# Ranking the products of Z C v with the first layer's weights in front of the next batch's attention

## The chip, the core and the metric

The kernel runs on one core of a Trainium2 chip. The metric is the device time of one execution in microseconds (us), the median of several runs. The engines are TensorE (PE in the rows, its weight loads PEld), VectorE (DVE), ScalarE (ACT), GpSimd (POOL) and SyncE (SP), which issues the DMA transfers. Every engine takes its instructions in the order in which the program lists them, and an instruction whose input is not there holds up all behind it.

## The reference

```python
C = sm(q_lm, k)                       # 32 landmarks per head
Z = iterated inverse of Bm            # 6 steps
attn = A @ Z @ C @ v                  # 4 batches, 8 heads, 576 x 64
x = attn.transpose(0, 2, 1, 3).reshape(2304, 512)
xn = x / sqrt(mean(x * x) + 1e-6) * rms_g
x = (silu(xn @ w_gate) * (xn @ w_val)) @ w_out    # 512 -> 1536 -> 512
# then a mixture of 8 experts, taken by the rows with x @ w_skip > 0
```

## The kernel before

The kernel never forms the attention's output. For a batch it computes the small matrix Z C v (32 landmarks by 64, for 8 heads), transposes it, scales it by `rms_g` and keeps it as `WT`. It multiplies `WT` with the first layer's weights: `product` makes a tile `P` of 128 x 512 for two groups of heads, which then plays the part of the weights, while the normed rows of A (`ap_t`) play the part of the activations. All large matrix products run in three pieces of split numbers (high part and low part, `rsplit`): for `P` ACT casts the PSUM bank to the high part and DVE subtracts it to get the low part.

The hidden layer is cut into thirds of 512 columns. A batch has six products: here g0, v0, g1, v1, g2, v2, for gate (g) and value (v) of thirds 0 to 2. Each takes 16 matmul instructions (32 in the trace, two passes each) on a quarter-sized piece of the array, 64 rows by 32 columns; `manual_schedule` fixes their order among themselves, so that eight pieces run side by side. Its results fill the two PSUM banks of the pool `pb`, which serve also the small steps `lp`, `lg` and `x2t` of the unit before. So the next product waits until both casts and both subtractions of the one before are done.

Its weights come through `load_w`: four DMA transfers of 256 KB on SP's queue, into the tiles `wl` (gate) or `wr` (value). There are two tiles of each, so the load of the next third waits until PE has finished the product with this one.

The main loop runs over eight units, two halves of 288 rows for each of four batches. A unit goes through 12 pieces of the hidden layer (`pg`, `pv`, 6 matmuls each, thirds 0 to 2 of `P` four pieces each), and then 144 matmuls of the output projection (`o`). Side work is woven in through generators: the next batch's attention (`attention`, from a batch's first half on), the products of the next batch (`products`, queued from piece 4 of the second half), and `finish` of the unit before. The steps of the attention that the prediction names are `gram`, `sq` (both the product with `gram` and, in the following batch, the scores), `ms`, `rbs` (the rows' norm: ACT takes a square root, which needs a table load on ACT), `ap` and `ap_t` (normed rows, split), then for the batch after that `s`, `lmk`, `bdq` (landmarks, on DVE), `pb`, `sq`, `mx`, `C`, `cT`, `sk`, `pv` with `vt`. Tanh for `h` needs ACT's other table.

What sets the final order on each engine is a scheduler that picks, among the instructions that it takes to be ready, the one of best rank. The rank is the place at which the program wrote it. I call the passage from one batch to the next a boundary: the first one lies at about 200 to 250 us, the second at 308 to 350, the third at 420 to 470.

Of the kernel before, what the change touches and what calls it, by code (L numbers as in the profile page):

```python
# [29 lines left out]
ROUND = 1.5 * 2.0**23  # L30
LP = 40
NC0 = 5
SLACK = 700


# [27 lines left out]
def attention_moe_kernel(  # L63
# [16 lines left out]
    def rsplit(lo_eng, hi, lo, src):  # L80

        A.copy(hi, src)
        lo_eng.tensor_tensor(lo, src, hi.bitcast(F32), ALU.subtract)
# [58 lines left out]
    def bank(name):  # L142
        return pb.tile([128, 512], F32, name=name, tag="b")
# [615 lines left out]
    def convert_w(i):  # L759

        load_raw(i)
        w = wo_tile(F32)
        from_f64(w, raws[i], wtile("s64"))
        for a in (1, 2):
            load_raw(i + a)
        SP.dma_start(parts_at(w_d[PARTS[i][0]], i), w)
        wparts[PARTS[i]] = w
# [13 lines left out]
    def load_w(n, q, last=False):  # L781

        ws = []
        for c in range(2):
            if n == "g" or last:
                w = wtile("wl").rearrange("p c n -> p (c n)")
            else:
                w = raw.tile([128, DM, 2], F32, name="wr", bufs=2)
                w = w.rearrange("p c n -> p (c n)")
            w = w.rearrange("p (i n) -> p i n", n=PC)  # L790
            f = DM * q + PC * c
            for g in range(2):
                SP.dma_start(
                    w[64 * g : 64 * g + 64],
                    w_d[n][256 * g : 256 * g + 256, f : f + PC].rearrange(
                        "(i p) n -> p i n", p=64
                    ),
                )
            ws.append(w)
        wparts[n, q] = ws  # L800
# [4 lines left out]
    def ptile(n, g, q):  # L805
        i = PIECES.index((n, g))
        return P_t[q][:, i, 0], P_t[q][:, i, 1]

    def product0(q, n, g):

        ps = bank("P")
        w = wparts.pop((n, g, q))
        for p in range(2):
            PE.matmul(
                ps[64 * p : 64 * p + 64, :], WTs[0][:, g, p],
                w[:, p], start=True, stop=True,
            )
        hi, lo = ptile(n, g, q)
        rsplit(V, hi, lo, ps)

    def product(b, q, n):

        pss = [bank("P") for g in range(2)]
        ws = wparts.pop((n, q))

        with tc.manual_schedule(engines={nc.tensor.engine}):
            for c in (1, 0):  # L830
                for i in range(KC):
                    for g in (1, 0):
                        gs = slice(64 * g, 64 * g + 64)
                        PE.matmul(
                            pss[g][32 * i : 32 * i + 32, PC * c : PC * c + PC],
                            WTs[b][gs, i], ws[c][gs, i], start=True, stop=True,
                        )
        for g, ps in enumerate(pss):
            hi, lo = ptile(n, g, q)
            rsplit(V, hi, lo, ps)  # L840

    def products(b, q):

        if b == 0:
            for n, g in PIECES:
                product0(q, n, g)
                yield
            return
        last = b == B - 1 and q == NQ - 1
        for n in "g" if last else "gv":  # L850
            if (n, q) not in wparts:
                load_w(n, q)
        for n in "gv":
            product(b, q, n)
            if last and n == "g":
                load_w("v", q, last)
                yield
            elif n == "g" and q < NQ - 1:
                load_w(n, q + 1)
            yield  # L860
# [167 lines left out]
    def pair_at(lst, i):  # L1028
        return ld(lst, i, E - 1), ld(lst, i + LP, B - 1)
# [156 lines left out]
    def slot():  # L1186
# [3 lines left out]
        for g in side[:]:  # L1190
            if max(busy[n] for n in "VAG") > busy["P"] + SLACK:
                break
# [47 lines left out]
    def first_convs():  # L1240
        for i in range(NC0):
            convert_w(i)
            yield
# [22 lines left out]
    ptile_q(1)  # L1266
    h_t = pool(ph1, "h_p").tile([128, FC, 2, NH], F32R, name="h_t")
    drain(products(0, 0))
    late_constants()
    fast = False  # L1270
# [4 lines left out]
    def conversions():  # L1275
        for i in range(NC0, 12):
            convert_w(i)
            yield
            if i == 7:
                drain(products(0, 1))  # L1280
                yield
        nonlocal raw
        start1.close()
        raw = pool(pha, "raw", side="right")
        ptile_q(2)
        drain(products(0, 2))
        yield
        side.append(att)
        for f in range(FC):
            convert_wout(f)  # L1290
            yield
# [24 lines left out]
    for u in range(1, 2 * B):  # L1316
        b, half = u // 2, u % 2
# [60 lines left out]
    with tc.For_i(0, npairs) as i:  # L1378
        e, b = pair_at(rest[0], i + 1)
# [36 lines left out]
```

## Time and profile before

| | us |
|---|---|
| median of 3 runs (711.12 to 711.8) | 711.46 |
| the profiled execution | 710.12 |
| its span, first to last instruction | 708.4 |
| PE busy | 650.1 (92%) |
| DVE busy | 459.8 (65%) |
| ACT busy | 295.4 (42%) |
| POOL busy | 145.1 (20%) |
| mean granted share of TensorE's clock | 0.96 |

A time of the profile is one execution's; the median of the runs is 1.34 above that execution. Busy PE is not PE at its best: a lone small matmul counts as busy while it runs through the array with nothing beside it.

### The profile page before, as it was taken

Reading aid. Unit: us, or ns where it says so; the run is one execution under the profiler, and the core shown is the slowest. Engines: PE = TensorE matmul, PEld = TensorE weight load, DVE = VectorE, ACT = ScalarE, POOL = GpSimd, SP = SyncE. Lnnn points to the kernel's source line nnn. Section 1 sums busy time; section 2 is a strip of 40 time slices with the busy share of each in tenths; the row PEclk is TensorE's granted clock in tenths of the full one; section 3 lists DMA queues with packets and bytes.
Section 4 is the critical chain, followed back from the end, with each engine's and each line's share of the span. In section 5 each row is a group of like instructions: output and inputs, shape, how many; then the busy total and the mean of one; then the engine's idle time right before and its main releaser. Section 6 shows DMA issues by size and latency. Waiting matters only on the chain.

```text
span 708.4 us, 13179 instructions
## 1 busy us (share of the span) xinstructions
PE 650.1 (92%) x4895; PEld 561.1 (79%) x4895; DVE 459.8 (65%) x1030; ACT 295.4 (42%) x637; POOL 145.1 (20%) x162
## 2 busy tenths in 40 slices
PE   5368599798998899999999999999989999999997
PEld 5256177687986598978899887999889988988985
DVE  5995999979877596878368768261452554352451
ACT  0873888834324431443341335240452244242340
POOL 4000035213200140220040030040372024022120
PEclk9775799999998999999999999999999999999999
DMA  8686644762238543428522108230451275445454
GB/s 295 229 256 223 218 148 160 215 171 83 67 95 182 123 111 86 132 64 201 134 66 68 66 20 170 67 73 1 161 153 64 60 234 197 150 130 175 134 158 147
DMA packets 79439, 97.17 MB, mean 137 GB/s; under 512 B 16016, under 2 KB 58000, under 8 KB 79376
## 3 DMA queue, kind: packets, MB, share of 16 engines
q1 hardware_dynamic: 79376, 96.33, 46.2%
q8 instruction: 39, 0.64, 0.4%
q14 instruction: 24, 0.20, 0.1%
HBM read 76.97 MB, written 19.34 MB: 136 GB/s over the span
## 4 chain that ended last, share of the span: by engine, by line
PE 70%; DVE 16%; DMA 4%; ACT 3%; issue 3%; POOL 2%; SPq 1%; POOLq 0%; ACTq 0%; DVEq 0%
PE o L58 17%; PE py L58 11%; PE ph L58 11%; PE pv L58 9%; PE pg L58 8%; PE P L58 3%; PE sq L58 3%; DVE wo L58 3%; PE nr L58 2%; DVE h L58 2%; DVE rbs L58 2%; DVE P L58 1%; PE sk L58 1%; DMA kq<-in_q_dram 1%; DVE ap L58 1%
## 5 line engine op out<-in xcount | busy, mean ns | idle before, releaser
L58 PE MATMUL o<-h_t,wo 128*128 128x288 f32 x1152 | 168.1, 301 | 6.5 <-ACT wo L58 3.6
L58 PEld LDWEIGHTS o<-h_t,wo 128*128 128x128 f32 x1152 | 157.3, 190 | 15.5 <-issue 5.9
L58 POOL TENSOR_TENSOR h_t<-h,h_t 128x288 fp32r<-128x288 f32 x96 | 81.6, 853 | 366.1 <-ACT h_t L58 343.8
L58 PE MATMUL pg<-ap_t,P 128*128 128x288 f32 x576 | 101.1, 305 | 10.8 <-ACT P L58 7.9
L58 PE MATMUL pv<-ap_t,P 128*128 128x288 f32 x576 | 102.4, 306 | 2.5 <-DVE h L58 2.1
L58 PEld LDWEIGHTS pg<-ap_t,P 128*128 128x128 f32 x576 | 83.1, 190 | 22.9 <-issue 14.8
L58 PEld LDWEIGHTS pv<-ap_t,P 128*128 128x128 f32 x576 | 83.8, 191 | 8.7 <-DVE h L58 4.3
L58 PE MATMUL ph<-xsh,P 128*128 128x288 f32 x384 | 78.1, 296 | 0.0
L58 DVE SCALAR_TENSOR_TENSOR h<-h,pg 128x288 f32<-128x288 f32 x96 | 42.6, 446 | 33.8 <-ACT h L58 33.2
L58 PEld LDWEIGHTS ph<-xsh,P 128*128 128x128 f32 x384 | 62.0, 188 | 0.6 <-issue 0.5
L58 ACT ACTIVATE h<-pg 128x288 f32<-128x288 f32 x96 | 39.2, 410 | 49.1 <-PE pg L58 46.4
L58 PE MATMUL ph<-xsl,P 128*128 128x288 f32 x192 | 56.9, 296 | 0.0
L58 ACT CAST h_t<-h 128x288 fp32r<-128x288 f32 x96 | 41.2, 431 | 30.2 <-DVE h L58 29.7
L58 PE MATMUL py<-wo,h_t 128*128 128x512 f32 x210 | 51.7, 397 | 0.0
L58 DVE TENSOR_TENSOR h<-h,pv 128x288 f32<-128x288 f32 x96 | 42.5, 446 | 7.7 <-PE pv L58 5.0
L58 PEld LDWEIGHTS py<-wo,h_t 128*128 128x128 f32 x210 | 39.5, 188 | 9.6
L58 DVE STREAM_TRANSPOSE T<-kq 64x576 f32<-64x576 f32 (+1 forms) x40 | 35.5, 887 | 5.1 <-DMA kq<-in_k_dram 4.0
L58 PEld LDWEIGHTS ph<-xsl,P 128*128 128x128 f32 x192 | 36.0, 188 | 0.1
L58 DVE TENSOR_TENSOR P<-P,P 128x512 fp32r<-128x512 f32 x48 | 31.6, 681 | 6.8 <-ACT P L58 6.5
L58 POOL TENSOR_TENSOR P<-w1r,P 128x512 fp32r<-128x512 f32 x16 | 21.2, 1329 | 69.0 <-ACT P L58 66.9
L58 ACT CAST P<-P 128x512 fp32r<-128x512 f32 x48 | 26.3, 587 | 21.7 <-PE P L58 21.1
L58 DVE TENSOR_SCALAR x2T<-o 128x288 f32<-128x288 f32 x16 | 7.3, 456 | 40.6 <-PE o L58 40.5
(235 smaller groups left out, 954.5 us busy)
## 6 DMA issues: line engine op xcount, KB each, us to landing
wl<-wg_d SPq DMA_DIRECT2D x36, 256.0 KB, 4.6
wr<-wv_d SPq DMA_DIRECT2D x32, 256.0 KB, 4.9
w1r<-in_moe_w_dram SPq DMA_DIRECT2D x32, 256.0 KB, 3.3
wr<-in_moe_w_gate_dram SPq DMA_DIRECT2D x6, 1024.0 KB, 6.3
wr<-in_moe_w_val_dram SPq DMA_DIRECT2D x6, 1024.0 KB, 5.9
wo<-in_moe_w_dram SPq DMA_DIRECT2D x24, 256.0 KB, 5.0
kq<-in_k_dram SPq DMA_DIRECT2D x8, 576.0 KB, 4.4
kq<-in_q_dram SPq DMA_DIRECT2D x8, 576.0 KB, 4.1
```

The lines of the kernel that those rows point to most:

```text
L58: return f(*args, **kw)
```

## The change

The two lines around `product` in `products` rank all that a product issues as though it had been written 150 places earlier. That holds for its matmuls, casts and subtractions. The loads of weights stay outside of the block. The first batch's products take another path and are not touched.

```diff
+AHEAD = 150
...
         for n in "gv":
-            product(b, q, n)
+
+            with tc.high_priority(offset=AHEAD):
+                product(b, q, n)
             if last and n == "g":
                 load_w("v", q, last)
                 yield
```

No instruction is added or taken away. What moves is shown for the places that the prediction speaks of.

First boundary, PE, from the norm of the second batch (`ms`) to its first hidden pieces. `P<-wl` is a gate product, `P<-wr` a value product; x16 is a whole one. Before:

```order
L58 MATMUL ms<-sq,onesd 128x288 x2
L58 MATMUL o<-h_t,wo 128x288 x2
L58 MATMUL P<-wl,WT 32x256 x16
L58 MATMUL o<-h_t,wo 128x288 x54
L58 MATMUL pg<-ap_t,P_675 128x288
L58 MATMUL P<-wl,WT 32x256 x16
L58 MATMUL pg<-ap_t,P_675 128x288 x5
L58 MATMUL P<-wr,WT 32x256 x16
L58 MATMUL pb<-lmk_2544,bdq 64x32 x2
L58 MATMUL sq<-T,bdq 64x288
L58 MATMUL pv<-ap_t,P_675 128x288 x2
```

After (two lone matmuls of g0 stand further ahead, in front of each pair of `sq`):

```order
L59 MATMUL P<-wl,WT 32x256 x14
L59 MATMUL o<-h_t,wo 128x288 x3
L59 MATMUL ms<-sq,onesd 128x288 x2
L59 MATMUL o<-h_t,wo 128x288 x44
L59 MATMUL P<-wl,WT 32x256 x16
L59 MATMUL o<-h_t,wo 128x288 x11
L59 MATMUL P<-wr,WT 32x256
L59 MATMUL o<-h_t,wo 128x288 x2
L59 MATMUL P<-wr,WT 32x256 x15
L59 MATMUL o<-h_t,wo 128x288 x10
L59 MATMUL pg<-ap_t,P_675 128x288 x6
```

g0 moves in front of `ms` and is cut in three; g1 and v0 move from the first hidden piece into the projection, and v0 is cut in two. On ACT the same place reads, before:

```order
L58 ACTIVATE x2T<-o 128x288
L58 ACT_TABLE_LOAD
L58 ACTIVATE rbs<-rbs,eps 128x288 x2
L58 CAST P_675<-P 128x512 x2
L58 CAST ap_t<-ap 128x288 x3
```

And after:

```order
L59 ACTIVATE x2T<-o 128x288
L59 CAST P_675<-P 128x512 x2
L59 ACT_TABLE_LOAD
L59 ACTIVATE rbs<-rbs,eps 128x288 x2
L59 CAST ap_t<-ap 128x288 x2
L59 CAST P_679<-P 128x512 x2
```

The table load and the square root now stand behind the casts of g0, and the casts of g1 between those of `ap_t`.

First boundary, PE, some 15 us later: the scores of the third batch's attention, with v1, g2 and v2. Before:

```order
L58 MATMUL sq<-T,bdq 64x288 x3
L58 MATMUL P<-wr,WT 32x256 x16
L58 MATMUL cT<-ident,C 96x128 x6
L58 MATMUL P<-wl,WT 32x256
L58 MATMUL sk<-T,bdk 64x288
L58 MATMUL P<-wl,WT 32x256 x15
L58 MATMUL sk<-T,bdk 64x288 x3
```

After:

```order
L59 MATMUL sq<-T,bdq 64x288
L59 MATMUL P<-wr,WT 32x256 x16
L59 MATMUL sq<-T,bdq 64x288 x3
L59 MATMUL P<-wl,WT 32x256 x16
L59 MATMUL cT<-ident,C 96x128 x6
L59 MATMUL lp<-x2T,wcat 32x288 x4
L59 MATMUL sk<-T,bdk 64x288 x4
```

v1 moves into the scores, and g2 follows it with only three `sq` between; g2 is whole again. The subtractions of v1 on DVE stand behind two reductions `mx` of these `sq`.

Second boundary, PE, g0 to g1. Before (two lone matmuls of g0 stand ahead of this, in front of two runs of `sq`):

```order
L58 MATMUL P<-wl,WT 32x256 x14
L58 MATMUL pg<-ap_t,P_984 128x288 x3
L58 MATMUL ms<-sq,onesd 128x288 x2
L58 MATMUL pv<-ap_t,P_984 128x288
L58 MATMUL P<-wr,WT 32x256
L58 MATMUL pv<-ap_t,P_984 128x288 x5
L58 MATMUL o<-h_t,wo 128x288 x3
L58 MATMUL P<-wr,WT 32x256 x15
L58 MATMUL o<-h_t,wo 128x288 x28
L58 MATMUL P<-wl,WT 32x256
L58 MATMUL o<-h_t,wo 128x288 x8
L58 MATMUL P<-wl,WT 32x256 x15
```

After:

```order
L59 MATMUL P<-wl,WT 32x256 x16
L59 MATMUL gram<-GT 128x128
L59 MATMUL sq<-AT,gram 128x288 x2
L59 MATMUL pg<-ap_t,P_984 128x288 x2
L59 MATMUL P<-wr,WT 32x256
L59 MATMUL pg<-ap_t,P_984 128x288
L59 MATMUL pv<-ap_t,P_984 128x288
L59 MATMUL P<-wr,WT 32x256 x15
L59 MATMUL sq<-AT,gram 128x288 x2
L59 MATMUL pv<-ap_t,P_984 128x288 x5
L59 MATMUL o<-h_t,wo 128x288 x14
L59 MATMUL P<-wl,WT 32x256 x16
```

g0 and g1 are whole now, v0 is still cut in two, and g1 stands closer behind g0. Behind this v1, cut in two before, is whole, and v2, whole before, is cut in two. The third boundary changes in the same way, except that v1 was whole there already.

## Rows read from the trace of the kernel before

**Rows 1.** The page's head

```profile
span 708.4 us, 13179 instructions
```

**Rows 2.** Busy time by stretch: stretch and length, then engine busy (x instructions), clock, DMA

```profile
180.00:240.00 60.00, 56.31 (x500) 45.91 (x500) 42.56 (x92) 20.32 (x49) 5.11 (x6) 0.94 0.49 120
...
300.00:360.00 60.00, 59.73 (x549) 50.13 (x548) 41.83 (x97) 24.14 (x56) 9.87 (x13) 1.00 0.55 131
...
420.00:480.00 60.00, 59.38 (x551) 50.45 (x550) 36.18 (x77) 23.86 (x56) 11.27 (x14) 1.00 0.40 92
```

**Rows 3.** The same view of three short stretches of the first boundary

```profile
218.90:221.70 2.80, 1.02 (x19) 0.47 (x25) 2.80 (x7) 2.02 (x3) 0.00 (x0) 1.00 0.99 299
221.80:228.50 6.70, 6.13 (x43) 4.38 (x29) 3.32 (x11) 1.51 (x5) 0.00 (x0) 0.50 1.02 210
...
235.00:237.50 2.50, 1.83 (x10) 0.84 (x10) 1.66 (x4) 2.08 (x6) 0.00 (x0) 1.00 0.75 195
```

**Rows 4.** Timeline of PE, first boundary: start, length, operation [idle before, releaser]

```profile
220.71 2.20 PE L58 MATMUL P<-wr,WT 64*32 64x256 f32 x32 [1.78 <-DVE P L58]
223.47 0.43 PE L58 MATMUL pb<-lmk,bdq 128*64 128x32 f32 x4 [0.57 <-DVE bdq L58]
...
234.96 1.01 PE L58 MATMUL cT<-ident,C 128*96 128x128 f32 x6 [0.48 <-ACT C L58]
236.64 0.62 PE L58 MATMUL P<-wl,WT 64*32 64x256 f32 x2 [0.67 <-DVE P L58]
```

**Rows 5.** Timeline of PE, second boundary

```profile
311.25 0.62 PE L58 MATMUL P<-wl,WT 64*32 64x256 f32 x2
311.79 1.24 PE L58 MATMUL sq<-AT,gram 128*128 128x288 f32 x4
...
323.65 0.62 PE L58 MATMUL P<-wl,WT 64*32 64x256 f32 x2
324.20 1.33 PE L58 MATMUL o<-h_t,wo 128*128 128x288 f32 x8
325.46 1.09 PE L58 MATMUL P<-wl,WT 64*32 64x256 f32 x30
```

**Rows 6.** Timeline of PE, third boundary

```profile
435.16 0.59 PE L58 MATMUL P<-wl,WT 64*32 64x256 f32 x2 [0.45 <-DMA wl<-wg_d]
...
440.86 1.09 PE L58 MATMUL P<-wr,WT 64*32 64x256 f32 x32
441.89 12.93 PE L58 MATMUL o<-h_t,wo 128*128 128x288 f32 x95
```

**Rows 7.** Timeline of SP's issues, second and third boundary

```profile
314.92 2.88 SPq L793 DMA_DIRECT2D wl<-wg_d  x4
...
425.93 2.60 SPq L793 DMA_DIRECT2D wl<-wg_d  x4
```

**Rows 8.** DMA issues, last of each of these four: count, size, us to landing

```profile
wl<-wg_d SPq DMA_DIRECT2D x1, 256.0 KB, 4.5
...
wl<-wg_d SPq DMA_DIRECT2D x1, 256.0 KB, 7.1
```

**Rows 9.** Groups by line: busy, mean ns of one, idle before and releaser

```profile
L58 DVE TENSOR_TENSOR P<-P,P 128x512 fp32r<-128x512 f32 x48 | 31.6, 681 | 6.8 <-ACT P L58 6.5
...
L58 ACT CAST P<-P 128x512 fp32r<-128x512 f32 x48 | 26.3, 587 | 21.7 <-PE P L58 21.1
```

**Rows 10.** Timeline of DVE, first boundary

```profile
233.00 0.94 DVE L58 TENSOR_REDUCE mx<-sq 128x1 f32<-128x288 f32 x2 [3.35 <-PE sq L58]
```

**Rows 11.** Timeline of ACT, first and second boundary

```profile
202.19 1.28 ACT L58 ACT_TABLE_LOAD   x1
208.26 1.02 ACT L58 ACTIVATE rbs<-rbs,eps 128x288 f32<-128x288 f32 x2 [4.79 <-DVE rbs L58]
...
316.74 1.28 ACT L58 ACT_TABLE_LOAD   x1
318.04 0.96 ACT L58 ACTIVATE rbs<-rbs,eps 128x288 f32<-128x288 f32 x2
```

## The prediction

> **What bounds the kernel now.** I read the busy times by stretch first. From the first boundary on PE is the bound: it is busy for 59.73 of 60 us around the second boundary and 59.38 around the third, at full clock [rows 2]. So at these two no more than 0.27 and 0.62 us of idle time can be won, and anything beyond that must come from PE doing the same work more densely. The first boundary is different: 56.31 of 60 us, at a mean clock of 0.94 [rows 2]. The short stretches say where. Between 218.9 and 221.7 us PE is busy for 1.02 of 2.80 us; from 221.8 to 228.5 its granted clock is 0.50, the lower level of 1.2 GHz, while it is busy for 6.13 of 6.70 us [rows 3]. The timeline names the waits: v0 starts after 1.78 us of idle time that ended with DVE's subtraction of g1, and `pb` after 0.57 us, waiting for DVE's landmarks [rows 4]. The products and the landmarks of the attention after next meet on DVE there, and PE stands still. That is the place at which the order can matter.
>
> **The change, first boundary.** What goes: g1 and v0 now stand in the projection, where other work runs while their banks are emptied. The idle 1.78 and 0.57 us go [rows 4]. If PE is busy before it, the clock doesn't fall; work of 6.13 us at half clock takes half at full clock, so 3.05 us go at most [rows 3]. Together 5.4.
>
> What comes, in four steps. (1) Cuts. A lone first matmul of a product takes 0.54 to 0.55 us from its start to the next instruction's (311.25 to 311.79, 323.65 to 324.20), and the rest of the product still takes what a whole one does: 1.03 for a whole one (440.86 to 441.89) [rows 5, 6]. The eight `o` behind it take 1.26 (324.20 to 325.46) and not 8 x 0.136 = 1.09, with 12.93 / 95 = 0.136 for one in a long run [rows 5, 6]. So a cut costs about 0.7. This boundary had one (g2) and gets three (two in g0, one in v0): 2 x 0.7 = 1.4. (2) v0 behind g1. An evacuation is two casts of 0.59 on ACT and two subtractions of 0.68 on DVE [rows 9]; the first bank is free 1.3 us after the product at the earliest, and between stand 11 `o`, 1.5 us. But ACT and DVE now take `ap_t` first, and that comes later than before: the table load ran at 202.19, hidden, 4.8 us before its square root at 208.26 [rows 11]; now it stands behind g0's casts, and the square root comes 1.5 to 2 us later. Walking down DVE's queue from there I get the first subtraction of g1 about 1.0 us after PE asks for the bank. Bounds 0 and 2.0. (3) `pv` of the first hidden piece needs the low part of v0. Ten `o` and six `pg` stand between, 2.2 us, against casts, subtractions and a few DVE steps of normed rows and landmarks: 0.6, bounds 0 and 1.5. (4) g2 close behind v1. Before, `cT` and g2 waited 0.48 and 0.67 us [rows 4]. Now DVE does `mx` twice (0.94) and two subtractions (1.36) before both banks are free [rows 9, 10], 2.3 us, while three `sq` give PE about 1 us of work: some 1.35 of waiting, and 0.8 for `lp`, which needs a bank of g2. That is 1.0 more than the 1.15 before; bounds 0 and 2.2. SP's queue loses nothing that PE waits for here: the `vt` loads behind the weights are wanted later.
> The sum is -5.4 + 1.4 + 1.0 + 0.6 + 1.0 = **-1.4**, between -5 and +1.7.
>
> Here a page speaks against the change. In the trace the square root starts 0.02 us after the table load of 1.28 us ends (316.74 + 1.28, 318.04) [rows 11]. The Trainium skill (ScalarE: Activation LUTs, What ACT_TABLE_LOAD costs) adds a drain of about 1.38 us to each switch, 2.66 in all. By that, step (2) would cost 2.4 and the whole change would save 2.7 us and not 4.05; these rows show no such drain, and I stay with 1.28.
>
> **Second boundary.** Before, it has five cuts (two in g0, one each in v0, g1 and v1), after it two (v0 and v2): -3 x 0.7 = -2.1. With the idle 0.27 us gone, -2.4. What may come is a wait for weights. The load of g1 starts when g0 frees its tiles: before, at 314.92; the last of the four transfers, issued some 0.65 before the end of their 2.88 us, at about 317.2, landed 4.5 later, at 321.7, that is 6.8 after the first issue [rows 7, 8]. Between g0 and g1 PE now has 23 full matmuls (23 x 0.136 = 3.1), four `sq` (two in at most 1.24 [rows 5], so about 2 for four), a `gram` (about 0.3) and the cut v0 (1.03 + 0.7): some 7.1 us, and g0 ends about 0.25 after the first issue. By this boundary's own landing that is just in time; by the third's it is 1.8 too early. I take 0, and keep 1.8 for the range. The table load and the `ap_t` chain are later here too, but the hidden pieces that need them still stand behind g2 and 72 `o`, 72 x 0.136 = 9.8 us, so they cost nothing; that cover gone, the 1.5 to 2 us of step (2) would show.
> **-2.4**, between -3.0 and -0.6.
>
> **Third boundary.** Four cuts become two: -1.4, and the 0.62 us of idle time [rows 2], 0.45 of them the wait for g1's weights [rows 6], go or are replaced. The weights: first issue at 425.93, the last at about 427.9, landed after 7.1, so 9.1 after the first issue, and indeed PE waited until 435.16 [rows 6 to 8]. The same 23 matmuls and small steps stand before g1 now, so PE asks 1.75 too early. I take this boundary's own landing: -1.4 - 0.6 + 1.75 = **-0.25**, between -2.0 and +0.5.
>
> All other instructions keep their order, and PE is busy behind each boundary, so what is won stays won. The sum is -1.4 - 2.4 - 0.25 = -4.05. Against the profiled execution's own time, 710.12 (708.4 of span [rows 1] and 1.7 around it), that is 706.1; the runs' median lies 1.34 above, so 707.4 for the median.
>
> **The rivals.**
> *Evacuation takes the place of order.* The four waits of the first boundary come out at their upper ends: products that follow each other closely wait for each other's casts and subtractions, which take 1.2 and 1.4 us against 1.03 on PE. Steps (2) to (4) cost 5.7 and not 2.6: 707.4 + 3.1 = 710.5, no change that can be told. For it: the largest wait of this boundary, 1.78 us, was one for a subtraction [rows 4]. Against it: all but v1 and g2 have now 1.5 us or more of other work between them. The Trainium skill (TensorEngine Tiling (Array Packing), PSUM Bottleneck) says that emptying PSUM may become the bound once small tiles run side by side; this is that case.
> *The clock falls at new waits: slower.* Before the fall at 221.8 PE had been idle for 1.78 of 2.80 us, with a narrow product behind [rows 3, 4]. Now g2's wait of 1.35, with `lp`'s 0.8 soon after, and the third boundary's wait of 1.75 for weights, with narrow products behind each, look much the same. One fall costs what the old one did, 3.05 us: 710.45. Two falls cost 6.1: 713.5, slower. It decides from two falls on, that is, if both waits reach about 1.8 us. Against it: between 235.0 and 237.5 PE was busy for 1.83 of 2.50 us, among narrow products, and the clock stayed at 1.00, the level of 2.4 GHz [rows 3].
> *The waits don't come.* DVE and ACT are ahead of my walk and the weights land in 6.8 us everywhere: steps (2) to (4) near 0.5 in all and no wait at the third boundary, 707.4 - 2.1 - 1.75 = 703.5.
> That the change does nothing is ruled out by the order.
>
> **How the numbers follow.** A measurement of this kernel can tell some 0.2% from no change, that is 710.04 to 712.88 for none. Forecast (705 to 709.5): 0.55. No waits (702 to 705): 0.12. Evacuation or one fall (710 to 711.5): 0.20, a fourth of it still below 710.04. Two falls or more, or the upper ends together: 0.13. So faster 0.72, same 0.15, slower 0.13. The range from 702.5 to 711.5 leaves out the slower case and the far end of the best one.
>
> **What would show it.** In the profile after: no clock of 0.50 around 220 to 230 us; v0's wait of 1.78 gone, and waits of about 1 us for DVE's `P` in the projection's end and at g2; no lone product matmuls among `sq` at the second and third boundary, and g0, g1 in one piece of about 1.03 us there; a wait of some 1.7 us for `wl` at the third. Wrong would be: a half clock at a new place, waits of DVE's `P` over 2 us, or a table load of ACT with PE waiting for `ap_t` behind it.

## The result and the profile after

| | before | after |
|---|---|---|
| median of the runs (8 each), us | 711.00 (706.74 to 711.80) | 703.98 (701.33 to 705.49) |
| ratio, 95% interval | | 0.9905 [0.9884, 0.9926] |
| the profiled execution, its span | 710.12, 708.4 | 704.12, 702.4 |

The change makes the kernel faster by 0.95%, about 6.75 us (the two medians are 7.02 apart). The prediction was 4.05 us and 707.4 for the median; its range, 702.5 to 711.5, holds the time, but its main case, 705 to 709.5 with a chance of 0.55, does not: 703.98 lies in the case without waits, which had 0.12. Two more measurements, on two chips and each beside its own runs of before, gave 0.9895 [0.9859, 0.9930] and 0.9902 [0.9868, 0.9936]. Here is the head of the page of after, with the line on PE, and the groups that answer to [rows 9].

```profile
span 702.4 us, 13192 instructions
...
PE 646.1 (92%) x4895; PEld 561.4 (80%) x4895; DVE 457.9 (65%) x1030; ACT 296.4 (42%) x637; POOL 144.6 (21%) x162
```

```profile
L59 DVE TENSOR_TENSOR P<-P,P 128x512 fp32r<-128x512 f32 x48 | 31.4, 687 | 1.6 <-ACT P L59 1.4
...
L59 ACT CAST P<-P 128x512 fp32r<-128x512 f32 x48 | 26.2, 588 | 22.3 <-PE P L59 21.8 <-DVE ap_t L59 0.3
```

PE is busy for 4 us less than before (650.1) with the same work: three cuts fewer, and no half clock at the first boundary. The evacuations take what they took; what went is idle time of DVE in front of the subtractions, from 6.8 to 1.6 us.

Busy time in the first stretch of [rows 2]:

```profile
180.00:240.00 60.00, 57.20 (x578) 45.81 (x574) 45.29 (x100) 21.89 (x53) 5.42 (x7) 1.00 0.55 131
```

PE is busy for 0.89 us more there and the clock is 1.00 throughout, where it was 0.94.

**Where the time went.** To divide it up I take a step that has the same place in all kernels, `lg` in every other unit, from the timeline of PE; here before, then after.

```profile
185.91 0.77 PE L58 MATMUL lg<-ident,h 128*128 128x9 f32 x6
...
288.04 0.67 PE L58 MATMUL lg<-ident,h 128*128 128x9 f32 x6
...
400.03 0.67 PE L58 MATMUL lg<-ident,h 128*128 128x9 f32 x6
...
502.86 0.67 PE L58 MATMUL lg<-ident,h 128*128 128x9 f32 x6
```

```profile
186.67 0.77 PE L59 MATMUL lg<-ident,h 128*128 128x9 f32 x6
...
285.15 0.67 PE L59 MATMUL lg<-ident,h 128*128 128x9 f32 x6
...
395.03 0.67 PE L59 MATMUL lg<-ident,h 128*128 128x9 f32 x6
...
496.43 0.67 PE L59 MATMUL lg<-ident,h 128*128 128x9 f32 x6
```

The three distances between them hold one boundary each. The table gives them for every kernel that was profiled (one execution each), and the timed ratio beside them. b_again is the kernel before once more, a_again and a_third are the changed kernel once more; the others are explained below.

| kernel | 1st boundary, us | 2nd, us | 3rd, us | ratio to before, 95% |
|---|---|---|---|---|
| before | 102.13 | 111.99 | 102.83 | 1 |
| b_again | 102.15 | 111.96 | 102.56 | |
| after | 98.48 | 109.88 | 101.40 | 0.9905 [0.9884, 0.9926] |
| a_again | 98.44 | 109.95 | 101.06 | 0.9895 [0.9859, 0.9930] |
| a_third | 98.49 | 109.46 | 100.80 | 0.9902 [0.9868, 0.9936] |
| e1_batch2 | 98.45 | 112.54 | 102.57 | 0.9957 [0.9935, 0.9978] |
| e2_batch34 | 102.67 | 110.25 | 102.02 | 0.9959 [0.9933, 0.9985] |
| e3_evac | 100.34 | 112.52 | 103.33 | 1.0019 [0.9995, 1.0043] |
| e4_matmul | 98.47 | 110.73 | 104.04 | 0.9960 [0.9933, 0.9987] |
| c_late500 | 101.48 | 109.88 | 101.27 | 0.9945 [0.9921, 0.9969] |
| s_ahead75 | 98.49 | 132.99 | 114.28 | 1.0302 [1.0260, 1.0343] |
| s_ahead600 | 95.51 | 109.60 | 101.62 | 0.9886 [0.9851, 0.9922] |
| s_q01 | 96.95 | 108.50 | 101.07 | 0.9844 [0.9810, 0.9878] |
| s_q01_2 | 95.50 | 108.54 | 101.30 | 0.9868 [0.9834, 0.9902] |

The two profiles of before agree within 0.3 us, the three of after within 0.6. By their means the first boundary gave 3.67 us (102.14 to 98.47), the second 2.21 and the third 1.61, 7.5 in all. The profiled pair alone gives 3.65, 2.11 and 1.43. The prediction had 1.4, 2.4 and 0.25: the second boundary was right, the first and third were too low. What lies outside the three distances is 1.2 us longer in the profile of after than in that of before; in the five profiles of the two kernels it lies anywhere between 389.3 and 393.8 us, so a single execution's whole span says less than these distances.

Busy time between the four marks, before:

```profile
185.91:288.04 102.13, 97.20 (x880) 81.85 (x881) 76.80 (x180) 32.55 (x84) 13.49 (x16) 0.97 0.48 120
288.04:400.03 111.99, 111.72 (x1011) 96.86 (x1010) 81.57 (x196) 41.41 (x106) 21.23 (x26) 1.00 0.41 105
400.03:502.86 102.83, 102.21 (x900) 92.02 (x899) 54.37 (x129) 34.34 (x88) 19.25 (x24) 1.00 0.27 67
```

And after:

```profile
186.67:285.15 98.48, 95.55 (x881) 80.22 (x881) 76.01 (x180) 32.92 (x84) 13.09 (x16) 1.00 0.50 125
285.15:395.03 109.88, 109.65 (x1011) 96.87 (x1010) 80.46 (x196) 41.33 (x106) 21.26 (x26) 1.00 0.42 106
395.03:496.43 101.40, 100.64 (x901) 92.22 (x899) 54.04 (x129) 34.89 (x88) 19.24 (x24) 1.00 0.29 68
```

At the first boundary PE's idle time fell from 4.93 to 2.93 us and its busy time from 97.20 to 95.55, at a clock of 1.00 where it was 0.97. At the other two there was hardly any idle time to win. What they gained is busy time, by denser work at an unchanged clock: 2.07 us for three cuts less and 1.57 for two, 0.69 and 0.79 a cut (a cut is a place at which other matmuls stand inside a product).

First boundary, timeline of PE, after; it answers to [rows 4]:

```profile
215.60 1.09 PE L59 MATMUL P<-wl,WT 64*32 64x256 f32 x32
...
218.94 0.62 PE L59 MATMUL P<-wr,WT 64*32 64x256 f32 x2 [0.59 <-DVE P L59]
...
233.63 1.69 PE L59 MATMUL P<-wl,WT 64*32 64x256 f32 x32 [1.19 <-issue]
...
236.75 0.69 PE L59 MATMUL lp<-x2T,wcat 128*32 128x288 f32 x8 [0.64 <-DVE P L59]
...
242.37 0.77 PE L59 MATMUL lg<-ident,h 128*128 128x9 f32 x6 [0.27 <-DVE P L59]
```

These are g1, the lone first matmul of v0, g2, and the two small steps that need a bank behind g2. PE's waits in this stretch are 0.59 + 1.19 + 0.64 + 0.27 = 2.69 us; no wait of `pv` for v0 stands there. For g2 the profile names no releaser; the timeline of DVE has the two subtractions of v1 in front of it:

```profile
232.85 1.28 DVE L59 TENSOR_TENSOR P<-P,P 128x512 fp32r<-128x512 f32 x2
```

The first of them (0.68 us) ends at 233.53 and g2 begins at 233.63; the second ends at 234.13. Until then g2 stands still, and PE counts as busy: its row is 1.69 us long, where a whole product's is 1.09. In before v0 stood in the same way inside its row of 2.20 us [rows 4]; the rest of that length is the half clock. Here are the matmuls of `P` alone in the first 0.6 us, of v0 before and of g2 after:

```profile
220.70:221.30 0.60, 0.59 (x2) 1.00 0.95 234
```

```profile
233.60:234.20 0.60, 0.57 (x2) 1.00 1.14 247
```

Two of 32 run in it, 25 in the first 0.6 us of a product that waits for nothing (g1 of before, from 216.97). So 0.6 us of waiting is hidden in busy time at each of these two places.

### The profile page after: what moved, and what is told of

Its sections match the earlier page's. It is cut to its first block, busy times and chain, and to the rows that moved or that the text cites. A ratio compares the mean times of both kernels' runs of the same rounds, so it can differ in the third digit from the quotient of the medians.

```text
span 702.4 us, 13192 instructions
## 1 busy us (share of the span) xinstructions
PE 646.1 (92%) x4895; PEld 561.4 (80%) x4895; DVE 457.9 (65%) x1030; ACT 296.4 (42%) x637; POOL 144.6 (21%) x162
## 4 chain that ended last, share of the span: by engine, by line
PE 72%; DVE 14%; DMA 4%; ACT 4%; issue 3%; POOL 1%; SPq 1%; ACTq 0%; POOLq 0%; DVEq 0%
PE o L59 18%; PE py L59 11%; PE ph L59 11%; PE pv L59 9%; PE pg L59 7%; PE P L59 3%; PE sq L59 3%; DVE wo L59 3%; PE nr L59 2%; DVE h L59 2%; DMA kq<-in_q_dram 1%; PE sk L59 1%; DVE rbs L59 1%; PE x2t L59 1%; DVE P L59 1%
## 5 line engine op out<-in xcount | busy, mean ns | idle before, releaser
L59 DVE SCALAR_TENSOR_TENSOR h_t<-ph,h_t 128x288 fp32r<-128x288 f32 (+2 forms) x45 | 14.6, 353 | 28.9 <-ACT h_t L59 28.9
```

The source lines that it names most:

```text
L59: return f(*args, **kw)
```

## The experiments

A product in three pieces has two cuts; before has 10 of them in the three boundaries (1, 5, 4), after 7 (3, 2, 2).

### One boundary without the others

The rank for the second batch alone (first boundary), and for the third and fourth alone (second and third boundary):

```diff
-            with tc.high_priority(offset=AHEAD):
+            with tc.high_priority(offset=AHEAD) if b == 1 else nullcontext():
```

> The rank only for the second batch's products, so only the first boundary (200 to 250 us) is changed; the second and third keep the order of before. Theory T (what the comparison of the two profiled runs says: the first boundary gave 3.6 us, the second 2.1, the third 1.4): 3.6 us less than before, a ratio near 0.995, about half of the whole gain of 6.7 to 7 us. The prediction's own sum for this boundary: 1.4 us less (ratio 0.998). Rival A, the change works through the second and third boundary alone and the first boundary's difference is drift between two executions: no difference, ratio 1.000.

```diff
-            with tc.high_priority(offset=AHEAD):
+            with tc.high_priority(offset=AHEAD) if b > 1 else nullcontext():
```

> The rank only for the third and fourth batch's products: the second and third boundary as in the changed kernel, the first as before, with its idle 1.78 us in front of the first third's value product and the half clock behind it. Theory T: 3.5 us less than before (2.1 + 1.4), ratio 0.995, and the first boundary's stretch at the half clock is there as before. The prediction's own sum: 2.65 us less. Rival A: all of the 6.7 to 7 us, ratio 0.9905. With the first kernel of this call: the two gains add up to the whole one if the boundaries do not act on each other.

Measured: 0.9957 and 0.9959 of 708.87, so 3.05 and 2.9 us less, each with an interval of about 1.5 to 2 us on either side. Together 6 us, so the boundaries add up, and half of the gain is the first one's; it is no drift. In the profiles the first kernel has after's length in the first boundary and before's in the others, the second the reverse, all within some 0.6 us.

### What of the rank does it: evacuations or matmuls

Only the casts and subtractions ranked ahead:

```diff
-        for g, ps in enumerate(pss):
-            hi, lo = ptile(n, g, q)
-            rsplit(V, hi, lo, ps)
+        with tc.high_priority(offset=AHEAD):
+            for g, ps in enumerate(pss):
+                hi, lo = ptile(n, g, q)
+                rsplit(V, hi, lo, ps)
```

> Only the evacuations (the casts and subtractions) are ranked ahead by 150, the products' matmuls keep the place of before. TensorE's order at the first boundary is that of before, so the products' cuts stay. Theory T: the evacuation of the first third's gate product no longer stands behind the landmark inverse's work on VectorE, so the idle 1.78 us and the half clock (3.05 us) go, and what waits for the landmarks pays about 1 us: 3 to 4 us less than before at the first boundary, nothing at the other two, ratio about 0.995. Rival B (the place of the matmuls carries the gain, the evacuations follow it): no difference, ratio 0.999 to 1.001. Rival C (evacuations in front hold up the attention that TensorE waits for next): slower by 1 to 2 us.

Only the banks and matmuls:

```diff
-        pss = [bank("P") for g in range(2)]
+        with tc.high_priority(offset=AHEAD):
+            pss = [bank("P") for g in range(2)]
...
-            with tc.high_priority(offset=AHEAD):
-                product(b, q, n)
+            product(b, q, n)
```

(the matmuls stand in the block too, the casts and subtractions don't)

> Only the products' matmuls and their banks are ranked ahead, the casts and subtractions keep the rank of before, so TensorE's order is about that of the changed kernel, with few cuts, but the first third's gate evacuation stands behind attention work on VectorE again. Theory T: the second and third boundary give their 3.5 us, the first boundary keeps its wait for a free bank (now earlier in the order, 2 us or more, as evacuations are later against the matmuls than before) and perhaps the half clock: 2 to 3.5 us less than before, ratio 0.995 to 0.997. Rival B (the place of the matmuls carries the gain): 6.7 us less, ratio 0.9905.

The evacuations' rank alone gives nothing: 1.0019 [0.9995, 1.0043]. My expectation fell here. The timeline of PE in e3_evac shows why: the wait in front of v0 is there, as long as before.

```profile
219.30 2.56 PE L59 MATMUL P<-wr,WT 64*32 64x256 f32 x32 [1.79 <-DVE P L59]
```

DVE's order in front of that wait is that of before: the better rank didn't bring g1's subtractions forward, probably because the scheduler doesn't take them to be ready any earlier (not shown). So the rank of the evacuations is not what removed the wait; what another place of theirs would do, this kernel doesn't test.

The matmuls' rank alone gives 0.9960. That is the time I expected, but not for the reason I gave: I had the gain at the second and third boundary and none of it at the first. In the profile the first boundary has the whole of it, 98.47 against 98.48. There it needs no help:

```profile
216.43 0.62 PE L59 MATMUL P<-wr,WT 64*32 64x256 f32 x2 [0.59 <-DVE P L59]
...
424.14 1.22 PE L59 MATMUL P<-wl,WT 64*32 64x256 f32 x32 [0.61 <-DMA wl<-wg_d]
...
432.69 0.66 PE L59 MATMUL o<-h_t,wo 128*128 128x288 f32 x3 [0.76 <-ACT h_t L59]
433.85 3.73 PE L59 MATMUL o<-h_t,wo 128*128 128x288 f32 x26 [0.50 <-POOL h_t L59]
```

In the second boundary it is 0.85 to 1.3 us behind after (one cut more, in v1), in the third 2.6 to 3.2: there `o` waits 1.26 us for `h_t`, and PE is idle for 2.61 us in all against 0.76 after. So the evacuations' rank is worth having, but only at the two later boundaries and only beside the matmuls' rank.

### Putting the wait back

After, with g1's evacuation at the first boundary ranked late, so that its second subtraction stands behind the landmarks:

```diff
-        for g, ps in enumerate(pss):
-            hi, lo = ptile(n, g, q)
-            rsplit(V, hi, lo, ps)
+        late = b == 1 and (n, q) == ("g", 1)
+        with tc.high_priority(offset=-500) if late else nullcontext():
+            for g, ps in enumerate(pss):
+                hi, lo = ptile(n, g, q)
+                rsplit(V, hi, lo, ps)
```

> The changed kernel, but at the first boundary the evacuation of g1 (the second product) is ranked 350 behind the program's order, so its second subtraction stands on VectorE behind the landmarks of the next attention, the value product of the first third waits for it again and the matmuls pv behind it. It puts back a suspected cost: the idle time in front of v0. Theory (idle of 1.8 us and more among narrow products brings the half clock here): the idle comes back, 2 us or more, the clock falls in the profile between 215 and 230 us, and the time is 3 to 6 us above the changed kernel's, ratio to before 0.994 to 0.999. Rival (the half clock of before has another cause than the wait): idle comes back, the clock stays at 1.00 there, and the time is 1 to 2.5 us above the changed kernel's.

It gives 706.43, 3.2 us above the changed kernel measured beside it (703.25), and in the profile the first boundary is 3.0 us longer than after's. But the clock stays at 1.00. Timeline of PE, then the stretch from 215 to 232 us:

```profile
223.66 0.31 PE L59 MATMUL pb<-lmk,bdq 128*64 128x32 f32 x4 [1.18 <-DVE bdq L59]
```

```profile
215.00:232.00 17.00, 14.39 (x145) 10.91 (x144) 13.38 (x35) 8.32 (x19) 1.51 (x2) 1.00 0.67 158
```

The scheduler answered by moving `pb` and three `sq` in front of all of v0 but its lone first matmul, so a single wait of 1.8 us never came about: the longest is 1.18. From g1 to `lg` the waits add up to 1.7 us more than after (4.39 against 2.69), and there is a cut more. The time is one that the theory names and the clock is the rival's, so neither holds as I wrote it. So the place of an evacuation matters when it is made worse; the half clock was not put back, and its cause is not settled by this kernel.

### The wait and the half clock

> The kernel before once more, for a second profile of its first boundary. Theory: the idle 1.78 us in front of v0 comes from the order and stands there again, and with it a half clock between 218 and 230 us, as in the three profiles so far that have this order there (6.9, 6.8 and 3.4 us of it). Rival (the fall is chance and only comes together with the wait by accident): the idle is there and the clock stays at 1.00.

The second profile of before has both, the wait in front of v0 and the half clock behind it, as well as the wait of `lg` that my sum left out:

```profile
219.44 2.16 PE L58 MATMUL P<-wr,WT 64*32 64x256 f32 x32 [1.78 <-DVE P L58]
...
239.88 0.69 PE L58 MATMUL lp<-x2T,wcat 128*32 128x288 f32 x8 [0.20 <-DVE P L58]
...
245.44 0.77 PE L58 MATMUL lg<-ident,h 128*128 128x9 f32 x6 [1.01 <-DVE P L58]
```

From 215 to 232 us the mean granted clock is 0.80 in before, b_again and e2_batch34, and 0.90 in e3_evac: in the four profiles with the order of before, the lower level of 1.2 GHz lasted 6.8, 6.8, 6.8 and 3.4 us. In the ten profiles with another order there it is 1.00 in that stretch. One of these ten, s_q01, has 3.4 us of the lower level a little later, at 236.0, after a wait of 1.49 and one of 0.58 us; s_ahead600 and s_q01_2 have the same two waits and none of it. So the lower level came with the wait of 1.78 in four profiles of four, and with shorter waits only now and then. The four share the whole order around the wait, though, so that the wait by itself brings it is not shown.

The timed runs, which have no trace, are in keeping with this by the mean granted clock of each: its median is 0.959 to 0.961 in the runs of before beside the experiments, 0.960 in e2_batch34 and e3_evac, and 0.963 to 0.965 in after, a_again, a_third, e1_batch2, e4_matmul and c_late500. The 3.4 us of e3_evac instead of 6.8 are most of what its first boundary is shorter by in the profile: 1.8 us, and half of the difference is 1.7. But that run, 707.78, is the fastest of its twelve and has the highest clock, 0.965, so it does not stand for the others.

### What a cut costs

Rank 75 in place of 150:

```diff
-AHEAD = 150
+AHEAD = 75
```

> Rank 75: TensorE's order cuts the products into 64 pieces in place of the changed kernel's 25 (46 cuts in place of 7), single matmuls alternating with other matmuls. It prices a cut: at the 0.7 us that the prediction took, 39 more cuts cost 27 us, so about 730 us, ratio to before 1.03. Rival (what a lone first matmul costs is its wait for the bank or is hidden, and a cut as such costs 0.1 us or nothing): 704 to 708 us, ratio 0.993 to 0.999.

732.57 against some 730 expected. At the third boundary the last product's matmuls alternate with single `o`, at a clock of 1.00:

```profile
465.82 0.62 PE L59 MATMUL P<-wl,WT 64*32 64x256 f32 x2
466.37 0.40 PE L59 MATMUL o<-h_t,wo 128*128 128x288 f32 x1
466.70 0.62 PE L59 MATMUL P<-wl,WT 64*32 64x256 f32 x2
...
478.94 0.62 PE L59 MATMUL P<-wl,WT 64*32 64x256 f32 x2
479.49 2.80 PE L59 MATMUL o<-h_t,wo 128*128 128x288 f32 x19
```

The 16 pieces and 15 `o` between take 479.49 - 465.82 = 13.67 us. A whole product takes 1.03 and 15 `o` in a run take 15 x 0.136 = 2.04, so the 15 cuts cost 10.6 us, 0.71 each. That is the prediction's 0.7, fifteen times in a row.

The Trainium skill (TensorEngine Tiling (Array Packing), Tiling Modes) says that a change of tiling mode drains the engine. The rows are in keeping with that but don't show a drain by itself: a piece takes 64 rows by 32 columns of the array and an `o` the whole of it, and the alternation adds both the changes from one to the other and the time of a piece that runs alone. The page has no price for the change; here the two changes of a cut cost at most 0.71.

### More room between the products

```diff
-AHEAD = 150
+AHEAD = 600
```

> The rank raised from 150 to 600. TensorE's order differs from the changed kernel's in the first boundary and in the order of the attention behind it: the first product whole (1 cut there in place of 3), 23 matmuls o between the second and third product in place of 11. Theory (the idle ahead of the third product is the time in which the second one's evacuation is not covered by other TensorE work): that idle, 0.59 us after the change, is nil, and two cuts less at 0.7: 2 us less than the changed kernel, ratio to before 0.988 to 0.990. Rival (the attention pushed back is missed later: landmark and merge steps wait): as the changed kernel or up to 2 us slower, ratio 0.991 to 0.995.

And the same for the first two thirds alone, the last third at its old rank:

```diff
-AHEAD = 150
+AHEAD = 600
...
-            with tc.high_priority(offset=AHEAD):
+            with tc.high_priority(offset=AHEAD) if q < 2 else nullcontext():
```

> Rank 600 for the first two thirds' products only; those of the last third keep the rank of before. The first boundary as with 600 for all; in the second and third boundary one cut each in place of two. Theory of the cuts (0.7 us each): 1.4 us less than 600 for all, ratio to before 0.986 to 0.988, if the last third's evacuations, which now come later, are not waited for. Rival: they are waited for, by the gate matmuls of that third (0.5 to 1 us at each of two or three boundaries): no gain over 600 for all.

> The changed kernel as it is, on the chip of the first four experiments, since kernels are to be compared beside one another. If the first and the second-and-third boundary add up (ratios 0.9957 and 0.9959): 0.9916, 6 us less than before. If the evacuations' rank adds nothing to the matmuls' (0.996): 0.996; if it adds what the traces of the third boundary show (the matmul-only kernel waits 0.76 and 0.50 us there for h_t and has one cut more): 0.9925 or better.

The changed kernel gave 0.9895 [0.9859, 0.9930] here, on another chip than that of the first four experiments, beside its own runs of before. That holds the 0.9916 of boundaries that add up and leaves out 0.996, so the evacuations' rank does add to the matmuls'.

Timeline of PE, s_ahead600: g1, then 23 `o`, then v0 without a wait, and later the longest of the new waits.

```profile
212.84 1.09 PE L59 MATMUL P<-wl,WT 64*32 64x256 f32 x32
...
217.13 0.62 PE L59 MATMUL P<-wr,WT 64*32 64x256 f32 x2
...
234.34 0.69 PE L59 MATMUL lp<-x2T,wcat 128*32 128x288 f32 x8 [1.49 <-DVE P L59]
```

Between g1 and v0, with 0.93 us of `pg`, PE waited 1.78 us for the bank; with 11 `o` (1.7 us) it waits 0.59, with 23 (3.3 us) not at all. The profile's first boundary is 2.97 us shorter than after's. But PE is idle there for 3.03 us, against 2.93 after, since new waits stand for the old one; what went is busy time, of which two cuts are 1.4, g2's shorter standing 0.5, and the rest is not explained. In the timed runs little of it is seen: 702.53 against 702.64 for a_again, with intervals of some 2.5 us on either side, so both readings of the expectation stay possible. Their mean granted clock, 0.9615 in the median against 0.965, would fit a lower level in some of them; no trace shows it. With the last third at its old rank, 699.98, all six runs at or below the lowest of a_again (701.14).

> Rank 600 for the first two thirds' products only, once more beside the changed kernel: theory (2 cuts less at the first boundary, 1 less at each of the others, 0.7 each, so 2.8 us less than the changed kernel): ratio to before 0.984 to 0.988. Rival (the earlier lead was the chip's spread): as the changed kernel.

> The changed kernel once more, to stand beside the other two of this call: ratio to before 0.989 to 0.992.

On another chip 699.88 against 703.25. Against the same runs of before that is 0.9868 and 0.9902, and 0.9844 and 0.9895 on the chip before; the lead over the changed kernel is 3.4 and 2.7 us. This version beats both kernels. The expectation of 2.8 us for four cuts less (3 left in place of 7) fits in the sum, not by boundary: against the mean of after, the profile of s_q01_2 has 3.0, 1.2 and -0.2 us less in the three, where two, one and one cut at 0.7 would be 1.4, 0.7 and 0.7.

## Why the prediction was right, and where it was off

**The first boundary: 3.67 and not 1.4 us.** The mechanism is the one described; the terms for what comes were too high in all, and some that go were left out. (1) The two cuts at 1.4 stand, and the idle time and half clock at 5.4 too: no lower level is granted there in any profile of after. (2) v0 waits 0.59, not 1.0. (3) `pv` doesn't wait for v0's low part: 0, not 0.6. (4) g2 waits 1.19 and stands 0.6 more inside its row, `lp` waits 0.64: 2.43 in all against 1.15 before, so 1.3 and not 1.0. Not in the sum were the 0.6 that v0 stood inside its row before, and the waits of `lp` (0.20) and of `lg` (1.02) in before, which became 0.64 (counted in (4)) and 0.27. With these: -5.4 - 0.6 + 1.4 + 0.59 + 0 + 1.28 - 0.20 - 0.75 = -3.68, and 3.67 were measured. That the sum closes so well owes something to luck: two estimates came out below the value taken and one above, and what v0's standing gave, g2's took back. The lower end that the prediction gave for this boundary, -5, doesn't follow from its bounds either; they give -5.4 + 1.4 = -4.0.

Not shown is the reading beside it, that the meeting of products and landmarks on DVE sets the wait. The timeline of DVE before has it: a landmark step `s` stands right in front of the subtractions for which v0 waits.

```profile
219.30 0.75 DVE L58 TENSOR_TENSOR s<-T 128x576 f32<-128x576 f32 x1
219.97 1.28 DVE L58 TENSOR_TENSOR P<-P,P 128x512 fp32r<-128x512 f32 x2
```

But e3_evac, which was to test it, changed the rank of the evacuations and not their place, and c_late500 shows only that a later place costs. What the rows show is that PE waits less, the more other work it has between two products: 1.78, 0.59 and 0 us of waiting with 0.93, 1.7 and 3.3 us of work. From the end of g1 to the start of v0 it was 2.72 us before (217.99 to 220.71) and is 2.32 after (216.62 to 218.94). So of the 1.19 us by which the wait shrank, 0.8 is more work in between and 0.4 a bank that was free sooner.

**The second boundary: 2.2 and 2.4.** Five cuts became two, and the wait for weights that I took at 0 was 0.23 us (0.26 in a_again, none in a_third). These are the products there, after:

```profile
307.25 1.09 PE L59 MATMUL P<-wl,WT 64*32 64x256 f32 x32
...
310.13 0.62 PE L59 MATMUL P<-wr,WT 64*32 64x256 f32 x2
...
316.15 1.22 PE L59 MATMUL P<-wl,WT 64*32 64x256 f32 x32 [0.23 <-DMA wl<-wg_d]
...
321.79 1.09 PE L59 MATMUL P<-wr,WT 64*32 64x256 f32 x32
```

**The third: 1.4 to 2.0 and not 0.25.** The term that failed is the wait for weights, 1.75 us. After, the timeline of SP has the first issue of g1's weights, and that of PE g1 and a later wait:

```profile
417.16 2.60 SPq L794 DMA_DIRECT2D wl<-wg_d  x4
```

```profile
425.49 1.22 PE L59 MATMUL P<-wl,WT 64*32 64x256 f32 x32 [0.44 <-DVE h L59]
...
457.32 0.66 PE L59 MATMUL x2t<-ident,x2T 128*128 128x128 f32 x4 [0.32 <-DVE P L59]
```

PE asks 7.9 us after the first issue (425.49 - 0.44 - 417.16), not 7.35, and waits 0.44; the profile puts that down to DVE's `h`, and whether the weights were there is not shown. In a_again and a_third g1 starts 7.84 and 7.85 after the issue without a wait. In e4_matmul, s_ahead600 and e2_batch34 the wait, there put down to the weights, was 0.61, 0.61 and 1.06 us, and g1 began 8.5 to 9.0 after the issue. So the wait is real and lies between 0 and 1.1 us; I had taken one landing of before, 9.1 us after the first issue, as the rule for this boundary, and let PE ask 0.5 us too early. With 0.44 and 0.32 the sum for this boundary is -1.4 - 0.62 + 0.76 = -1.26, against 1.43 in that profile.

**The rivals.** Evacuation did not take the place of order: steps (2) to (4) cost 1.9 us, against 2.6 in the sum and 5.7 in this rival. The clock did not fall at the new waits of 1.19 and 0.64 us. In the profile of after it fell once from 180 us on, at 505.8, after waits of 0.53 and 1.26 us for `h` in a stretch that the change doesn't touch; the six matmuls `pv` behind took 1.81 us there and 1.06 in a_third, which has similar waits (0.57 and 1.02) and no fall. The case without waits came closest, 703.5 against 703.98, by another division: the waits did come, but smaller.

The Trainium skill (ScalarE: Activation LUTs, What ACT_TABLE_LOAD costs) would have a table switch cost 2.66 us. The timeline of ACT, after, again shows the square root right behind the load (209.39 + 1.28 = 210.67):

```profile
209.39 1.28 ACT L59 ACT_TABLE_LOAD   x1
210.69 0.96 ACT L59 ACTIVATE rbs<-rbs,eps 128x288 f32<-128x288 f32 x2
```

No drain is seen in it, and the smaller gain that would follow from one didn't come.

## What to carry to other kernels

Where one engine is busy throughout, ask how densely it works: a narrow matmul that stands alone among others cost 0.7 us more than in its group, and that price, read from two rows, held over 39 further cuts. Where a product waits for its predecessor's banks, give the engine other work between the two before you touch the evacuation; ranking the evacuations alone left their place in DVE's order and did nothing, ranking the matmuls alone gave all of the first boundary's gain, and ranking only the first two thirds, but higher, gave some 3 us more. A wait can stand inside busy time: compare the length of a row with that of the same work elsewhere. Price a wait for a transfer from several landings, from the first issue to the first use, and not from one.

## What the runs showed of the hardware

In s_ahead75 the granted clock was 0.50, the lower level, for 20.5 us at the second boundary, while PE was busy throughout, with single product matmuls and single `o` in turn. The same alternation at the third boundary ran at 1.00. Stretches of s_ahead75, the one ahead of the fall first:

```profile
330.00:338.90 8.90, 8.90 (x48) 5.55 (x46) 1.87 (x6) 0.52 (x2) 0.00 (x0) 1.00 0.53 118
338.90:359.40 20.50, 20.50 (x52) 9.90 (x53) 1.84 (x3) 1.17 (x2) 0.00 (x0) 0.50 0.21 52
458.00:478.00 20.00, 20.00 (x122) 11.46 (x121) 2.26 (x5) 1.49 (x3) 0.00 (x0) 1.00 0.28 60
```

So the lower level was granted without idle time in the 8.9 us in front of it, in the last 5 of which narrow and full matmuls took turns, and the same work didn't always bring it. The prediction took it that a busy PE keeps its clock; that held at the first boundary and not here. This profiled run took 738.42 us; it and the run of 736.38 have mean granted clocks of 0.955 and 0.954, the other four, 729.1 to 732.61 us, 0.965 to 0.967, so the lower level is part of the kernel's spread. What decides between the two levels stays open.
